# C of the first two pairs by block loads and a VectorE transpose, with other orders around these pairs

## The chip, the cores and the metric

The kernel runs on one core of one Trainium2 chip. The metric is the device time of one execution in microseconds (us). Three runs of the kernel before gave 364.21, 364.57 and 366.34 us; the median is 364.57.

The engines have short names in all tables: PE is TensorE (matrix products), PEld its weight loads, DVE is VectorE, ACT is ScalarE, POOL is GpSimd, and SP is the engine that issues most transfers (DMAs). A name with a q (SPq, DVEq) is the engine's instruction queue.

## The reference

Two stages follow each other. The first is a state-space layer in chunks (4 batches, 8 heads, 768 tokens, head size D = 32, state size N = 16); the second is a two-layer network with a PReLU between its layers.

```python
for c in range(nc):                                  # chunks of 32 tokens
    la = log_a[:, :, sl]; cum = np.cumsum(la, axis=-1)
    L = np.exp(cum[:, :, :, None] - cum[:, :, None, :]) * causal
    M = np.einsum('bhin,bhjn->bhij', Cc, Bc) * L
    y_intra = np.einsum('bhij,bhjd->bhid', M, xc)
    y_inter = np.einsum('bhin,bhnd->bhid', Cc, state) * np.exp(cum)[:, :, :, None]
    y[:, :, sl] = y_intra + y_inter
    Bx = np.einsum('bhjn,bhjd->bhjnd', Bc, xc) * decay_from_j[:, :, :, None, None]
    state = decay_full[:, :, None, None] * state + np.sum(Bx, axis=2)
x = y.transpose(0, 2, 1, 3).reshape(3072, 256)
h = x @ w_in                                         # 256 x 2048
g = np.maximum(h, 0.0) + alpha * np.minimum(h, 0.0)
out = g @ w_out                                      # 2048 x 256
```

The product of C and B of a chunk, before it is multiplied by the decays, is called the gram below. The chunk size of the reference is free: any split of the tokens gives the same result.

## The kernel before

**Tiling.** The 3072 tokens are 24 chunks of 128 tokens, and two neighbouring chunks are a pair (`gp`, 0 to 11). Two pairs, 512 tokens, make a group of the network. Tensor tiles have 128 partitions: B and C with tokens on the partitions (`nat`), or, turned, with head and state index on the partitions (`bc`, whose first half is B and second half is C). `cz` holds C twice, with the odd or the even heads set to zero, so that one matrix product with a 32-row strip gives the gram of two heads. `cd` is C times the decay products `pf`. `dec` holds the decays of a pair, made by scans on VectorE, and is then multiplied by the gram (`times`). `bn` is B times the decays towards the chunk's end; `added` multiplies it with x, and `states` makes the running states from these sums. `mask` sets the parts of a state that belong to other heads to zero. `x_products` and `state_products` give y, and `copy_out` brings it to `xT`, the input of the network.

**The order of work** is written out by hand: every engine runs its instructions in the order in which the program issues them. `first_two` (L818) holds the pairs 0 and 1, in chunks of 64 tokens. It spreads the raw decays to all rows by TensorE (`spread`, into four PSUM banks `sp`), scans them there (`scan`, L867), makes the gram into the other half of the same banks (`gram_of`, L876) and multiplies (`times`, L881). In between it converts the first weight pieces and runs the first parts of the network (`hidden_two`, L1081: two rows of hidden units for 256 tokens; its `rest` is the PReLU, ACT L1099 and DVE L1110). After `first_two` the loop over `f` from 4 to 15 takes the rest of the hidden units of group 0: `hidden(0, f)` (PE L1074, PReLU in ACT L1077 and DVE L1078), the stages of the pairs 2 and 3 (`ssm`), conversions, and `output(f - 4)` (PE L1121). The later groups follow in `quad`.

**Weights** come as 16 pieces of 512 KB, alternating from `w_in` and `w_out`, and each is converted on the way: ACT takes an absolute value (L269), DVE or POOL clamps it (L274), DVE takes the sign (L292), ACT makes a second part (L279, or L282 for `w_out`, which needs `g_mul` and `g_add` from `slope_signs`, L393), DVE combines (L302), and POOL adds (L324). `convert_a`, `sign`, `convert_b` and `convert_next` issue these steps. Six raw buffers exist, and `convert_next` issues the load of a later piece (L253).

**Transfers** are issued by SP in program order, and SP waits where a transfer needs an earlier one. Three results pass through DRAM so that they can be read back to all partitions: `short` (decay products of pair 1; written at L972, read by `load_second`, L227), `z` (decays for the scans of the pairs from 2 on; `rows_out`, L469, read by `load_spread`, L160), and `pf` (decay products from pair 2 on; `rows_products`, L439, read by `load_products`, L167). At pair 2 the state is first multiplied with such a product at L639.

**PSUM** has eight banks: two for tag `hp` (`spare`, `hidden` and the later `quad`), two for `ss`, and four named banks (`bank(0)` to `bank(3)`). `ss_tile` hands out the `ss` buffers and banks in turn by a counter, `early[0]`. Pair 2's gram takes three buffers of `ss_tile` and one of `spare` (`small = 3`).

**Warming.** `keep_warm` issues products without use to keep TensorE busy.

## Time and profile before

The table is of one profiled execution. It took 363.67 us, and its span on the core is 362.0 us.

| stretch, us | PE busy | DVE busy | ACT busy | POOL busy | granted PE clock | DMA share | GB/s |
|---|---|---|---|---|---|---|---|
| 0 to 30.88 | 24.21 | 23.66 | 13.80 | 17.05 | 1.00 | 0.84 | 178 |
| 30.88 to 51.86 | 20.51 | 15.06 | 11.10 | 11.73 | 0.92 | 0.83 | 233 |
| 51.86 to 362.0 | 306.67 | 200.19 | 146.12 | 173.39 | 1.00 | 0.28 | 64 |
| whole | 351.40 | 238.92 | 171.01 | 202.17 | 0.995 | | 84 |

Each row gives the busy time of an engine in a stretch of the span, the share of full speed that TensorE's clock was granted, the mean busy share of the 16 DMA engines, and what they moved. The first stretch ends where `hidden(0, 4)` starts, and the second where `output(4)` starts. A wait is named in the profile by the instruction that waited, an arrow, and the last instruction it seems to have waited for. In the list of an engine's instructions in order of time, the columns are the start, the duration, the engine, the line, the operation, what it writes and reads, and how many are merged into the row.

### The profile page before, as it was taken

To read this page: it belongs to the slowest core of one execution; us is meant where nothing else is said; L and a number is where in the kernel's file an instruction comes from. 1 tells how busy PE (TensorE), PEld (TensorE's weight loads), DVE (VectorE), ACT (ScalarE), POOL (GpSimd) and SP (SyncE) were. 2 spreads that over 40 slices of the span, in tenths; PEclk is the share of its full clock that TensorE was granted. 3 is DMA by queue.
4 is the path that set the end of the run, shared out by engine and by line. 5 is a ranking of instruction groups with operands and counts; after the bars stand their busy time and mean duration, and the time that the engine had idled before them with its cause. 6 is when DMAs were issued, how large, how long until landed. Compare 5 with 4: busy or idle time off the path is not lost.

```text
span 362.0 us, 7766 instructions
## 1 busy us (share of the span) xinstructions
PE 351.4 (97%) x2981; PEld 284.0 (78%) x2981; DVE 238.9 (66%) x489; ACT 171.0 (47%) x386; POOL 202.2 (56%) x224
## 2 busy tenths in 40 slices
PE   7887999999999999999999999999999999999996
PEld 3564656668888888888888888888888888888885
DVE  7976595989846756866656856657856634743363
ACT  3446656544355445535535535535535544453431
POOL 5656457669965947545546545537545546334510
PEclk9998999999999999999999999999999999999999
DMA  6899689704535421510530530530201001001102
GB/s 115 181 188 333 218 179 315 165 2 77 170 66 141 79 53 34 100 45 14 113 82 21 103 84 18 103 86 20 56 2 29 2 2 29 2 0 31 32 0 58
DMA packets 105581, 30.24 MB, mean 84 GB/s; under 512 B 79896, under 2 KB 101448, under 8 KB 105544
## 3 DMA queue, kind: packets, MB, share of 16 engines
q1 hardware_dynamic: 105160, 29.57, 35.6%
q8 instruction: 23, 0.38, 0.4%
q10 hardware_dynamic: 384, 0.18, 0.2%
q14 instruction: 14, 0.11, 0.1%
HBM read 26.32 MB, written 3.42 MB: 82 GB/s over the span
## 4 chain that ended last, share of the span: by engine, by line
PE 86%; DVE 4%; DMA 4%; SPq 2%; POOL 1%; ACT 1%; issue 1%; DVEq 0%; POOLq 0%
PE bank L1195 33%; PE hp L1220 28%; PE bank L1121 6%; PE ss L1220 6%; PE hp L1074 3%; DMA pf<-rpf 2%; PE ss L784 1%; DMA raw<-in_moe_w_in_dram 1%; DVE dec L564 1%; PE ss L728 1%; PE bank L1188 1%; DVE wr L302 1%; PE ss L776 1%; PE ss L802 1%; DMA ap<-pf 1%; POOL w_in L324 1%
## 5 line engine op out<-in xcount | busy, mean ns | idle before, releaser
L1277 POOL TENSOR_TENSOR gt<-gt 128x512 f32<-128x512 f32 x58 | 74.1, 1278 | 21.1 <-DVE gt L1205 16.3
L1195 PE MATMUL bank<-gt,w_out 128*128 128x256 f32 x320 | 83.5, 381 | 0.0
L1195 PEld LDWEIGHTS bank<-gt,w_out 128*128 128x128 f32 x320 | 60.1, 190 | 9.2 <-issue 1.0
L1205 DVE SCALAR_TENSOR_TENSOR gt<-hp,s_mul,gt 128x256 f32<-128x256 f32 x96 | 42.0, 479 | 29.0 <-ACT gt L1203 26.8
L1267 POOL TENSOR_TENSOR gt<-gt 128x512 f32<-128x512 f32 x20 | 25.4, 1269 | 62.6 <-DVE gt L1205 50.2
L1203 ACT ACTIVATE gt<-hp,s_alpha 128x256 f32<-128x256 f32 x96 | 40.3, 471 | 34.6 <-PE hp L1220 31.5
L1195 PE MATMUL bank<-gt,ws 128*128 128x256 f32 x224 | 55.9, 379 | 0.0
L1195 PEld LDWEIGHTS bank<-gt,ws 128*128 128x128 f32 x224 | 42.3, 190 | 5.6
L1220 PE MATMUL hp<-xs,w_in 128*128 128x256 f32 x160 | 41.9, 384 | 0.0
L1220 PE MATMUL hp<-xs,ws 128*128 128x256 f32 x160 | 41.1, 380 | 0.0
L1246 DVE TENSOR_TENSOR hp<-hp,u 128x512 f32<-128x512 f32 x20 | 14.0, 700 | 35.2 <-ACT u L1244 35.2
L1220 PEld LDWEIGHTS hp<-xs,ws 128*128 128x128 f32 x160 | 30.3, 190 | 4.3 <-POOL xs L1162 0.2
L1220 PEld LDWEIGHTS hp<-xs,w_in 128*128 128x128 f32 x160 | 29.7, 190 | 4.5
L1121 PE MATMUL bank<-w_out,gt 128*128 128x256 f32 x128 | 31.1, 385 | 0.4 <-POOL w_out L324 0.4
L1121 PEld LDWEIGHTS bank<-w_out,gt 128*128 128x128 f32 x128 | 23.6, 190 | 7.2 <-issue 3.1
L1074 PE MATMUL hp<-xT,w_in 128*128 128x512 f32 x48 | 24.5, 635 | 2.3 <-DVE gt L1110 2.3
L1220 PE MATMUL ss<-xT,w_in 128*128 128x256 f32 x96 | 24.6, 379 | 0.0
L642 POOL TENSOR_TENSOR sm<-state,bmask 128x256 f32<-128x256 f32 (+1 forms) x10 | 6.2, 621 | 32.1 <-DVE state L639 32.1
L558 DVE TENSOR_TENSOR_SCAN dec<-abc,bank 128x192 f32<-128x192 f32 x48 | 22.7, 523 | 0.0
L1235 ACT COPY m<-hp 128x512 f32<-128x512 f32 x8 | 4.7, 586 | 35.7 <-PE hp L1220 35.7
L1244 ACT COPY u<-hp 128x512 f32<-128x512 f32 x20 | 11.7, 585 | 19.4 <-PE hp L1220 19.4
L1205 DVE SCALAR_TENSOR_TENSOR gt<-c,s_mul,gt 128x256 f32<-128x256 f32 x40 | 20.6, 555 | 0.0
(234 smaller groups left out, 608.0 us busy)
## 6 DMA issues: line engine op xcount, KB each, us to landing
abc<-z SPq DMA_DIRECT2D x24, 192.0 KB
raw<-in_moe_w_in_dram SPq DMA_DIRECT2D x8, 512.0 KB
raw<-in_moe_w_out_dram SPq DMA_DIRECT2D x8, 512.0 KB
abc<-z SPq DMA_DIRECT2D x8, 512.0 KB
out_dram<-o_sb SPq DMA_DIRECT2D x32, 64.0 KB
nat<-in_B_dram SPq DMA_DIRECT2D x26, 64.0 KB
nat<-in_C_dram SPq DMA_DIRECT2D x24, 64.0 KB
xt<-in_x_dram SPq DMA_DIRECT2D x12, 128.0 KB
```

What stands on the lines that cost most here:

```text
L558: nc.vector.tensor_tensor_scan(out=dv[:, o : o + SQ], data0=abc[k][:, s : s + SQ], data1=ident_p[0][:, :SQ], initial=0.0, op0=ALU.mult, op ...
L642: nc.gpsimd.tensor_tensor(out=sm[:, :nk].rearrange("p k (g m) -> p k g m", g=2), in0=new[:, :nk].unsqueeze(2).to_broadcast([P, nk, 2, 2 * D]),
L1074: nc.tensor.matmul(hp, w_in[:, k, f * P : (f + 1) * P], xts[g][:, k], start=(k == 0), stop=(k == KC - 1))
L1121: nc.tensor.matmul(pos[0][t // 2][:, t % 2], gt[:, t * Q : (t + 1) * Q], w_out[:, f], start=(f == 0 and t % 2 == 0), stop=(f == NF - 1), s ...
L1195: nc.tensor.matmul(ms[g][i][:, h], w, blocks[g, z][n][:, p], start=(q == 0 and h == 0), stop=(q == NQ - 1), skip_group_check=True)
L1203: nc.scalar.mul(o[:, p], h[:, p], s_alpha[:, fs[p]])
L1205: nc.vector.scalar_tensor_tensor(out=o[:, p], in0=h[:, p], scalar=s_mul[:, fs[p]], in1=o[:, p], op0=ALU.mult, op1=ALU.max)
L1220: nc.tensor.matmul(to[:, p], w(2 * z + p), b, start=start and p == 0, stop=True, skip_group_check=True)
L1244: nc.scalar.copy(out=u2, in_=A)
L1246: nc.vector.tensor_tensor(out=Y, in0=Y, in1=u2, op=ALU.add)
L1267: nc.gpsimd.tensor_tensor(out=tc_, in0=g22, in1=g12, op=ALU.subtract)
L1277: eng.tensor_tensor(out=o, in0=x0, in1=x1, op=ALU.subtract)
```

## The change

C of the pairs 0 and 1 is no longer loaded with tokens on the partitions in runs of 64 bytes (one token of one head). It is loaded in blocks of 8 tokens of one head, 512 bytes, as the kernel already does for later pairs (`load_blocks`); VectorE then turns 32x32 blocks (`turned_c`), and ScalarE makes `cz` from the turned copy in SBUF (`spread_c`). TensorE still turns B (`turned_b`). `rows_short` is cut in two: the second scan and the write of `short` (`rows_begun`) come after the products of pair 0, with `load_second` and the loads of pair 2 behind them, while the loads of pair 1 go ahead. `gram_of` fills the banks 0 and 1 first. Two clamps and `first_a` of pair 1 go from VectorE to GpSimd, the clamp of weight piece 1 too; the copies of y go from VectorE to ScalarE. `slope_signs` comes earlier. Pair 1's sums, states and gram are issued ahead of `hidden_two(0, 2, 0)` instead of within it. The last `hidden_two` before the loop writes `bank(2)` instead of an `hp` buffer, and the counter of `ss_tile` starts at 17 instead of 16. Two uses of `keep_warm` are shortened or left out.

```diff
--- before.py
+++ after.py
@@ -181,14 +181,25 @@
             load_products(gp, ap)
         if gp == 0:
             load_rows(0, nc.scalar)
-            nc.sync.dma_start(out=al_n, in_=moe_alpha.rearrange("(k p) -> k p", p=P))
         abc = []
         later = []
+        def load_blocks(o, src, e):
+            first = src[b, e : e + 1, c * Q : (c + 2) * Q, :]
+            nc.sync.dma_start(out=o, in_=bass.AP(tensor=first.tensor, offset=first.offset,
+                                                 ap=[[2 * S * N, P // 32], [8 * N, 32], [1, 8 * N]]))
+        for e in range(2 if gp < NB else 0):
+            load_blocks(nat[:, 1, e], C, e)
+        if gp == 0:
+            nc.sync.dma_start(out=al_n, in_=moe_alpha.rearrange("(k p) -> k p", p=P))
         for k in range(2 if gp < HALF else 0):
             ts = slice((c + k) * Q, (c + k + 1) * Q)
-            for i, src in enumerate((B,) if turned else (B, C)):
+            for i, src in enumerate((B,) if turned or gp < NB else (B, C)):
                 nc.sync.dma_start(out=nat[:, i, k].rearrange("p (h n) -> p h n", h=H),
                                   in_=src[b, :, ts, :].rearrange("h p n -> p h n"))
@@ -207,12 +218,8 @@

...
@@ -477,21 +484,24 @@
-    def rows_short(r, rows):
-        clamp(nc.vector, starts_r[:RW, ::HQ], rows[:, ::HQ])
+    def rows_short(r):
         nc.vector.memset(r[:, ::HQ], 0.0)
         pr = lent[3][:RW, 2]
         nc.vector.tensor_tensor_scan(out=pr[:, ::-1], data0=r[:, 1:][:, ::-1],
                                      data1=ends_q[:RW, ::-1], initial=0.0, op0=ALU.mult,
                                      op1=ALU.add)
+        return pr
+    def rows_begun(r):
         rpf = lent[3][:RW, 3]
         nc.vector.tensor_tensor_scan(out=rpf, data0=r[:, :Q], data1=starts_r[:RW], initial=0.0,
                                      op0=ALU.mult, op1=ALU.add)
         scratch["short", 0] = dr.tile([RW, Q], F32, name="short0")
-        held["short"] = rpf
-        return pr
+        nc.sync.dma_start(out=scratch["short", 0], in_=rpf)
     def rows_turn(i, pr):
@@ -831,25 +841,24 @@
-        def turned(nat, tp, by):
-            for i in range(2):
-                for k in range(2):
-                    nc.tensor.transpose(tp[:, (2 * i + k) * P : (2 * i + k + 1) * P],
-                                        nat[:, i, k], ident)
+        def turned_c(nat):
             bc = work.tile([P, 4, Q], F32, name="bc")
+            nc.vector.transpose(
+                bc[:, 2:].rearrange("p k t -> p (k t)").rearrange("p (c b) -> p b c", b=8),
+                nat[:, 1].rearrange("p e (b n) -> p b e n", n=N))
+            return bc
+        def spread_c(bc):
             cz = czp.tile([P, 2, 2, Q], F32, name="cz")
-            flat = bc.rearrange("p i t -> p (i t)")
-            cs = slice(2 * Q, 4 * Q)
-            nc.scalar.copy(out=flat[:, : 2 * Q], in_=tp[:, : 2 * Q])
             for e in range(2):
-                o = cz[:, e].rearrange("p k t -> p (k t)")
-                if e and by is nc.vector:
-                    nc.vector.tensor_scalar(out=o, in0=tp[:, cs], scalar1=par[:, e : e + 1],
-                                            scalar2=None, op0=ALU.mult)
-                else:
-                    nc.scalar.mul(o, tp[:, cs], par[:, e : e + 1])
-            nc.scalar.copy(out=flat[:, cs], in_=tp[:, cs])
-            return bc, cz
+                nc.scalar.mul(cz[:, e].rearrange("p k t -> p (k t)"),
+                              bc[:, 2:].rearrange("p k t -> p (k t)"), par[:, e : e + 1])
+            return cz
+        def turned_b(nat, tp, bc):
+            for k in range(2):
+                nc.tensor.transpose(tp[:, k * P : (k + 1) * P], nat[:, 0, k], ident)
+            nc.scalar.copy(out=bc[:, :2].rearrange("p k t -> p (k t)"), in_=tp[:, : 2 * Q])
@@ -868,14 +877,16 @@
                                          initial=0.0, op0=ALU.mult, op1=ALU.add)
         def gram_of(bc, cz, banks):
-            for k in range(2):
-                for r in range(4):
-                    rs = slice(32 * r, 32 * r + 32)
-                    for j, hs in enumerate(halves):
-                        o = banks[r][hs, (2 + k) * Q : (3 + k) * Q]
-                        nc.tensor.matmul(o.rearrange("p (e t) -> p e t", e=2), bc[rs, k, hs],
-                                         cz[rs, :, k, hs], start=True, stop=True,
-                                         tile_position=(32 * r, HQ * j), skip_group_check=True)
+            for v in range(2):
+                for k in range(2):
+                    for r in (2 * v, 2 * v + 1):
+                        rs = slice(32 * r, 32 * r + 32)
+                        for j, hs in enumerate(halves):
+                            o = banks[r][hs, (2 + k) * Q : (3 + k) * Q]
+                            nc.tensor.matmul(o.rearrange("p (e t) -> p e t", e=2), bc[rs, k, hs],
+                                             cz[rs, :, k, hs], start=True, stop=True,
+                                             tile_position=(32 * r, HQ * j),
+                                             skip_group_check=True)
         def times(i, r, t):
             nc.vector.tensor_tensor(out=dec[i][:, r], in0=t[:, 2 * Q :], in1=dec[i][:, r],
@@ -941,7 +952,7 @@
                 o = xts[0][:, w, 2 * i * Q : 2 * (i + 1) * Q].rearrange(
                     "p (k j t) -> p j k t", k=2, j=2)
                 nc.scalar.copy(out=o[:, 0], in_=y[w][0])
-                nc.vector.tensor_copy(out=o[:, 1], in_=y[w][1])
+                nc.scalar.copy(out=o[:, 1], in_=y[w][1])
@@ -961,89 +972,91 @@
             for c in cs:
                 mask(i, slice(c, c + 1))
         rows = loads["r", 0]
         rq = prep.tile([RW, Q + 1], F32, name="rq")
         clamp(nc.vector, rq[:, :Q], rows)
         z0 = first_a(ap0, nc.vector, lent[1][:, :2])
+        clamp(nc.gpsimd, starts_r[:RW, ::HQ], rows[:, ::HQ])
+        clamp(nc.gpsimd, starts_a[:, ::HQ], ap0[:, ::HQ])
         sp = [bank(r) for r in range(4)]
         spread(z0, sp)
-        prq = rows_short(rq, rows)
-        clamp(nc.vector, starts_a[:, ::HQ], ap0[:, ::HQ])
-        nc.sync.dma_start(out=scratch["short", 0], in_=held.pop("short"))
+        prq = rows_short(rq)
+        bc0 = turned_c(nat0)
         load_pair(1)
-        load_second()
         nat1, _, xt1, pf1 = loads["p", 1]
         for r in range(4):
             scan(0, r, sp[r])
         rows_turn("short", prq)
         tp = spare()
-        bc0, cz0 = turned(nat0, tp, nc.vector)
+        cz0 = spread_c(bc0)
+        turned_b(nat0, tp, bc0)
+        slopes(alpha)
+        bn0 = pair_loads(0)
+        hp = spare()
+        keep_warm(hp, 1)
+        gram_of(bc0, cz0, sp)
+        dps = dps_in([hp, tp])
+        added(dps, bn0, xt0)
+        for r in (0, 1):
+            times(0, r, sp[r])
         nc.vector.tensor_tensor_scan(out=pf0, data0=z0.rearrange("p k t -> p (k t)"),
                                      data1=starts_a, initial=0.0, op0=ALU.mult, op1=ALU.add)
-        bn0 = pair_loads(0)
-        slopes(alpha)
+        z1 = first_a(loads["a", 1], nc.gpsimd, lent[1][:, 2:])
+        cd0 = decayed_c(bc0, pf0)
+        states(0, dps, pf0)
+        one_at_a_time(0, range(3))
+        for r in (2, 3):
+            times(0, r, sp[r])
+        rows_begun(rq)
+        load_second()
         rows_clamp(0)
         rows_out(0)
         load_next(2)
         load_pair(2, False)
         load_next(2)
         load_spread(2, *divmod(4, CPB))
-        cd0 = decayed_c(bc0, pf0)
-        hp = spare()
-        keep_warm(hp, 1, GT)
-        gram_of(bc0, cz0, sp)
-        dps = dps_in([hp, tp])
-        added(dps, bn0, xt0)
-        for r in (0, 1):
-            times(0, r, sp[r])
-        states(0, dps, pf0)
-        one_at_a_time(0, range(3))
-        for r in (2, 3):
-            times(0, r, sp[r])
-        z1 = first_a(loads["a", 1], nc.vector, lent[1][:, 2:])
         convert_a(*pieces[0], by=nc.vector)
         convert_b(*pieces[0])
         y = places([ss(), ss()], [hp, tp])
-        x_products(y, xt0, 0, (0,))
+        x_products(y, xt0, 0)
+        state_products(y, 0, cd0)
         sp = [bank(r) for r in range(4)]
-        keep_warm(sp[0], 1, GT)
-        x_products(y, xt0, 0, (1,))
-        state_products(y, 0, cd0)
         spread(z1, sp)
         keep_warm(sp[3][:, 2 * Q :], 1)
         convert_next()
         xts[0] = xtp.tile([P, KC, GT], F32, name="xT")
         copy_out(0, y)
-        convert_a(*pieces[1], by=nc.vector)
+        prelu_of = {0: hidden_two(0, 0, 0, spare())}
+        convert_a(*pieces[1])
+        bc1 = turned_c(nat1)
+        sign(*pieces[1])
+        scan(1, 0, sp[0])
         convert_b(*pieces[1])
-        prelu_of = {0: hidden_two(0, 0, 0, spare())}
+        for r in range(1, 4):
+            scan(1, r, sp[r])
+        bn1 = pair_loads(1)
+        convert_next(first=False)
+        cz1 = spread_c(bc1)
+        own = [ss(), ss()]
+        turned_b(nat1, own[0], bc1)
+        dps = dps_in(own)
+        added(dps, bn1, xt1)
+        slope_signs()
+        mask(0, slice(3, 4))
+        cd1 = decayed_c(bc1, pf1)
+        states(1, dps, pf1)
+        gram_of(bc1, cz1, sp)
+        one_at_a_time(1, range(3))
         for r in range(4):
-            scan(1, r, sp[r])
-        convert_next(first=False)
-        bn1 = pair_loads(1)
-        mask(0, slice(3, 4))
-        own = [ss(), ss()]
-        bc1, cz1 = turned(nat1, own[0], nc.scalar)
-        dps = [t.rearrange("p (k m) -> p k m", k=2)
-               for t in (own[1][:, 2 * Q : 2 * Q + 4 * D], sp[0][:, : 4 * D])]
-        cd1 = decayed_c(bc1, pf1)
+            times(1, r, sp[r])
+        prelu_of[0]()
+        convert_a(*pieces[2])
+        sign(*pieces[2])
         def among(i, k):
-            if (i, k) == (0, 0):
-                added(dps, bn1, xt1)
-                states(1, dps, pf1)
-            if (i, k) == (0, 1):
-                gram_of(bc1, cz1, sp)
-                one_at_a_time(1, range(3))
-                for r in range(4):
-                    times(1, r, sp[r])
-                prelu_of[0]()
-                convert_a(*pieces[2])
-                sign(*pieces[2])
             if (i, k) == (1, 0):
                 y = places(own, [bank(0), bank(1)])
                 x_products(y, xt1, 1)
@@ -1054,14 +1067,13 @@
         convert_b(*pieces[2])
         convert_next(first=False)
         mask(1, slice(3, 4))
-        slope_signs()
         prelu_of[2]()
         held["pr"] = rows_scan(0)
         rows_products()
         load_products(NB, loads["p", NB][3])
         state[0] = new[1][:, 3]
         masked[0] = sm[1][:, 3]
-        early[0] = 16
+        early[0] = 17
@@ -1418,7 +1430,7 @@
     sign(*pieces[3])
     hidden_two(0, 0, 2 * Q, spare())()
     convert_next(first=False)
-    rest = hidden_two(0, 2, 2 * Q, spare())
+    rest = hidden_two(0, 2, 2 * Q, bank(2))
     rows_turn(0, held["pr"])
     convert_a(*pieces[4])
     rest()
```

More of the change, by code (lines that the diff above doesn't have):

```diff
@@ L211, in load_pair @@
             for e in range(2):
-                first = src[b, e : e + 1, c * Q : (c + 2) * Q, :]
-                nc.sync.dma_start(out=nat[:, 1 + e, i],
-                                  in_=bass.AP(tensor=first.tensor, offset=first.offset,
-                                              ap=[[2 * S * N, P // 32], [8 * N, 32], [1, 8 * N]]))
+                load_blocks(nat[:, 1 + e, i], src, e)
         for k in range(2 if gp >= NB else 0):
```

## The prediction

> **What bounds the kernel now.** I read the waits of TensorE over the whole execution first: they show where the bottleneck engine stands still. The page has it busy for 351.4 of 362.0 us, so only stops can be won. Columns: us in total, times, longest.
>
> ```profile
> PE hp L1074 <- DVE gt L1110: 2.3, 1, 2.3
> PE hp L1089 <- POOL w_in L324: 1.2, 2, 0.9
> PE bank L876 <- DVE gt L904: 0.9, 1, 0.9
> ...
> PE bank L876 <- DVE cz L847: 0.5, 1, 0.5
> PE bank L1121 <- POOL w_out L324: 0.4, 1, 0.4
> ```
>
> All stops lie before 52 us. The last row is the one at 51.4 to 51.86 us, before `output(4)`. From there to the end the groups of TensorE show no other releaser. **So the total is the time at which TensorE gets past 51.86 us, plus 310.1 us that the change doesn't touch.** Second, TensorE in order of time around the largest stop, and the stretches with the granted clock (the number after the busy times, ahead of DMA share and GB/s):
>
> ```profile
> 28.32 0.25 PE L499 MATMUL ss<-ident,pr 96*128 96x96 f32 x1
> 30.88 3.63 PE L1074 MATMUL hp<-xT,w_in 128*128 128x512 f32 x4 [2.32 <-DVE gt L1110]
> ...
> 36.54 1.88 PE L1074 MATMUL hp<-xT,w_in 128*128 128x512 f32 x4
> ```
>
> ```profile
> 32.00:33.00 1.00, 1.00 (x2) 0.42 (x2) 1.00 (x2) 0.09 (x1) 0.92 (x2) 0.50 1.13 339
> 33.00:34.00 1.00, 1.00 (x2) 0.23 (x1) 0.49 (x2) 0.00 (x0) 0.92 (x2) 0.50 1.13 377
> ```
>
> `hidden(0, 4)` waits 2.32 us for its PSUM buffer, then takes 3.63 us instead of 1.88, at half clock: 4.07 us lost in one place. It looks like the prize. Third, the chain of waits from 33 to 52 us says whether it is one:
>
> ```profile
> 33.21 6.02 DMA pf<-rpf
> ...
> 39.24 2.62 DMA ap<-pf
> ...
> 41.96 0.28 DVE state L639
> 42.24 2.33 DVE dec L564 x4
> ...
> 45.69 0.66 DVE gt L1078
> 46.35 2.33 DVE dec L564 x4
> 48.68 0.64 DVE gt L1078
> ...
> 50.53 1.28 POOL w_out L324
> ```
>
> This chain runs beside TensorE. The decay products of pair 2 go out to DRAM, come back to all partitions, and only then can VectorE do pair 2's first state (L639). Behind it, in VectorE's order, stand two sets of scans, two PReLUs (L1078), and the conversion of the weights for `output(4)`, without a gap from 41.96 to 50.46 us. TensorE needs these PReLUs: pair 2's gram for heads 6 and 7 takes the `hp` buffer that the PReLU ending at 46.35 frees (that matmul starts at 46.41), `hidden(0, 8)` the next one. TensorE and this chain arrive within 0.44 us of each other at 51.86. **There are two bounds; shortening only TensorE's side wins 0.44 us at most.**
>
> Fourth, what sets the chain's start. VectorE has `rpf` ready at 27.5 us, but SP issues pf at 33.21. SP in order of time (start, duration):
>
> ```profile
> 9.62 3.48 SPq L192 DMA_DIRECT2D nat<-in_B_dram  x1
> ...
> 17.09 0.43 SPq L253 DMA_DIRECT2D raw<-in_moe_w_in_dram  x1
> ...
> 27.73 3.82 SPq L253 DMA_DIRECT2D raw<-in_moe_w_in_dram  x1
> ```
>
> Other loads of these kinds take 0.4 to 0.6 us, so SP is held inside the issue. The waits name ACT L269 for the 3.82 us, but the raw buffer being reused was last read by ACT at 12.6 us; a full queue fits better. The stretch from 28 to 38 us has a DMA share of 0.98 at 335 GB/s, and from 38 to 40 only 0.04: the queue drains and pf is its last item. So pf lands when the transfers issued since 17.09 us are done; these are seven weight pieces, pair 2's tensors and the spread rows, none of them changed.
>
> **What the Trainium skill says.** "TensorE: Matmul & The Clock Gate", Part 1: the clock halves after an idle window of about 3.4 us and returns after a busy one. The trace agrees on half clock (0.50) for some 3.4 us (0.51 from 31 us, 0.79 in 34 to 35), and shows that a 2.3 us stop was enough. Same page, Architectural detail: VectorE is a strict FIFO; L639 holding up the ready conversions agrees. "DMA: Bandwidth & Descriptors", Specifications: full rate needs 512 bytes per row. Agreed: 95 GB/s at 3 to 6 us (mostly 64-byte rows), 335 GB/s in the stretch above. Same page, Rules for kernel authors: a load of what an earlier DMA wrote waits for its completion; SP waits 5.5 us here for pf before ap.
>
> **The change, part by part.** Times are those of the profiled execution: span 362.0 us, run 363.67, median 364.57 (0.90 above it). I forecast a difference and add it to the median.
>
> *C in blocks.* For pairs 0 and 1, 2 x 2 loads of 64 KB go from 64-byte to 512-byte rows. At the measured rates 128 KB takes 1.35 us at 95 GB/s and 0.39 at 335: about 1 us less DMA per pair. Issues stay six per pair. For pair 0 C is issued first and B about 1 us later, so B's second half lands near 6.8 instead of 6.1 us. The first weight piece is still issued near 6.62 and lands at 11.0 to 11.3 instead of 11.35.
>
> *VectorE's transpose.* Two new ones of 128x256. The nearest row, L571, is 128x512 at 1.11 us; half is 0.55 us each (0.43 to 1.1 as bounds: L1371's 128x256 took 0.43). Removed from VectorE: L847 0.48, two clamps 0.35 + 0.14, pair 1's `first_a` 0.49 (L431, 128x252), piece 1's L274 0.41, four output copies 1.13. Net about 1.9 us less on VectorE. TensorE loses four transposes of C, two warming matmuls of 512 columns (1.03 and 1.13 us). ACT gains four copies of 0.27, loses two of 0.37. POOL gains two small clamps, a 252-wide clamp (0.65 for 127 columns, so 0.7 to 1.3) and piece 1's L274 (0.61); it idles 1.88 and 1.49 us before its L324s there, which covers them.
>
> *Gram 0.* It waited for cz L847 until 8.22. Now: C lands near 4.6, transpose to 5.2, two ACT scalings to 6.5, B's copy to 7.5, gram at 7.6. 0.6 us earlier, hidden behind the first weight piece (usable 14.66, now 14.2 to 14.6).
>
> *Pair 1's loads ahead of `short`; `load_second` after pair 0's times.* `rows_begun` ends near 11 us instead of 4.95. SP then issues `short`, and `load_second` waits for it to land. Queued ahead of `short` are pair 1's B and x, 4096 rows: the same kind of queue that held SP 3.48 us. Before, all of pair 1 was moved by about 17 us; now 1 us less work gives 15.5 to 16. `short` lands 0.4 us later (as ap followed pf's drain), `load_second` takes 0.78, z 0.42 to 1.13: the next weight piece is issued at 16.8 to 18.0 instead of 17.09. Behind it on SP stand all that pf waits for. **Shift of the gate: -0.3 to +0.9 us; I take 0.** The microsecond saved in transfers is spent on an empty queue during the round trip through DRAM. If neither appeared, DMA work alone would allow -1.5.
>
> *Pair 1.* Its ap lands near 18.3 as before, so the states start at 18.6 to 19.3 (18.94). The gram no longer follows them (-0.9 us of TensorE), four products L881 (1.42) and state products follow: xT complete near 23.9 instead of 24.53. -0.6.
>
> *`slope_signs` early, `bank(2)`.* ACT L282 no longer waits 1.90 us for POOL g_add; `hidden(0, 4)` takes a buffer freed one step earlier. The 2.32 us stop and the half clock go. It starts near 27.7, ends at 29.4 at full clock, instead of 34.5: TensorE is about 5 us ahead. Late next: pieces 3 to 5, whose conversions now end at about 29.8, 32.3 and 34.9, when TensorE asks at 29.4, 34.8 and 36.5; 0.4 us of wait. (Piece 3: ACT free of `copy_out` and a PReLU at 24.8, L269 0.6, L282 1.12, a scaling 0.87, then DVE L1110 and L302 to 28.5, POOL L324 1.27; POOL then adds 2.5 us a piece: L274 0.61, L324 1.27, and `bn` of pair 2 once.)
>
> *Where the 5 us go.* TensorE finishes `hidden(0, 7)` near 41, reaches the gram that needs L1078's buffer, and stands until 46.4 + shift: 5 us idle. That is longer than the 2.3 us that halved the clock, so it restarts at half clock. From 46.4 to 51.86 it has 1.0 (gram) + 1.73 (`output(3)`) + 1.96 (`hidden(0, 8)`) of work, with 0.5 us of slack. With 3.4 us at half clock 1.7 us of work are lost, less the slack and the 0.44: **about +0.9 us** (0 if the clock holds, 3.5 if `hidden(0, 8)` is cold too).
>
> Sum: 0 (gate) + 0.9 (cold restart) = +0.9: 364.57 + 0.9 = 365.5.
>
> **Rivals.** A, above: 364.7 to 366.7, chance 0.50. *B, the gate moves a little:* one or two bubbles in the queue vanish (share 0.09 in 25 to 26 us), pf lands up to 1.5 us earlier, the clock mostly holds: 363.0 to 364.7. For it: fewer rows in the queue; against it: `short`'s round trip. 0.25. *C, slower:* `load_second`, at SP's head, waits for `short` behind x of pair 1, the gate moves +1 us or more, and the restart stays cold for over 5 us, through `hidden(0, 8)`: +1 + 3.5 = 369.0, from 366.7 on. It decides from the point where the half clock outlasts the gram and `output(3)`, 5.5 us cold. For it: the stop is twice as long as the one that cost 3.4 us. 0.19, half of it beyond 1%. *D, the chain isn't a bound:* pf is issued as early as ACT or VectorE allow, as the named releaser L269 would mean, and TensorE keeps its 5 us: 359.6. Against it: 0.98 DMA share for ten microseconds. 0.06. *That the gram doesn't get behind the scans* changes nothing: the first weight piece covers it.
>
> **Numbers.** A change within 1% (3.65 us) can't be told from none here. Faster by over 1%: D, 0.06. Slower by over 1%: half of C, 0.10. Within: 0.84. Range 362.9 to 368.0: A, B and the lower part of C.
>
> **What would show it.** Right: `hidden(0, 4)` before 29 us at full clock; ap<-pf landing within 1 us of 41.87; a new wait of TensorE of 4 to 6 us on VectorE's L1078 in the gram L739, followed by clock 0.50. Wrong: pf issued before 31 us, or TensorE passing `output(4)` before 50 us; then DMA was not what held pf.

## The result and the profile after

The changed kernel takes **368.87 us** (median of six runs, 367.42 to 369.94); the kernel before, measured beside it, 364.45 (364.17 to 366.34). The ratio is 1.011, 95% interval 1.007 to 1.014: slower by about 4.4 us, where I had forecast +0.9 and a range that ended at 368.0. All ratios are taken over fast executions alone and lie near the ratio of their means, so for a kernel whose times fall into two groups they differ from the ratio of the medians. The profiled execution after took 369.63 us, 0.76 above its median, the one before 363.67, 0.78 below its own; so the two traces lie 5.9 us apart in span, some 1.5 us more than the medians.

The head of the page after: span, busy times, and the granted clock and DMA share in 40 slices of 9.2 us.

```profile
span 367.9 us, 7755 instructions
PE 355.5 (97%) x2975; PEld 288.2 (78%) x2975; DVE 237.9 (65%) x481; ACT 171.4 (47%) x389; POOL 206.0 (56%) x229
PEclk9799958999999999999999999999999999999999
DMA  5669778920724530430540540540300001001102
```

TensorE has six matmuls fewer in the trace than before and is busy 4.1 us longer. That isn't more work: the clock row shows where its matmuls are stretched, in the second slice (9 to 18 us) and in the sixth and seventh (46 to 64). Next, the largest wait of TensorE after (us in total, times, longest; the second largest is 1.3):

```profile
PE hp L749 <- DVE gt L1090: 3.4, 1, 3.4
```

The 2.3 us stop of `hidden(0, 4)` is gone, and a stop of 3.4 us stands in pair 2's gram, on the PReLU that was L1078 and is L1090 now: the wait that the prediction named as next. TensorE in order of time after shows both ends of it:

```profile
30.32 1.91 PE L1086 MATMUL hp<-xT,w_in 128*128 128x512 f32 x4
...
33.20 1.99 PE L1133 MATMUL bank<-w_out,gt 128*128 128x256 f32 x8 [0.54 <-POOL w_out L331]
...
49.68 0.79 PE L749 MATMUL hp<-cz,bc 32*128 32x256 f32 x1 [3.41 <-DVE gt L1090]
...
51.68 3.78 PE L1133 MATMUL bank<-w_out,gt 128*128 128x256 f32 x8
55.26 2.92 PE L1086 MATMUL hp<-xT,w_in 128*128 128x512 f32 x4
58.01 1.89 PE L1133 MATMUL bank<-w_out,gt 128*128 128x256 f32 x8
```

The end of the same stretch before (gram, `output(3)`, `output(4)`):

```profile
45.68 0.48 PE L739 MATMUL ss<-cz,bc 32*128 32x256 f32 x1
...
46.41 0.48 PE L739 MATMUL hp<-cz,bc 32*128 32x256 f32 x1
...
47.46 1.99 PE L1121 MATMUL bank<-w_out,gt 128*128 128x256 f32 x8
...
51.86 1.99 PE L1121 MATMUL bank<-w_out,gt 128*128 128x256 f32 x8 [0.44 <-POOL w_out L324]
```

`hidden(0, 4)` runs at full clock (1.91 us instead of 3.63), and `output(0)` starts at 33.20, 1.6 us ahead of before. Then all of that is lost and more: `output(4)` starts at 58.01 instead of 51.86. The 6.15 us there are the whole 5.9 us of the span, within 0.3. The chain of waits in the changed kernel says what TensorE stood for:

```profile
36.08 6.28 DMA pf<-rpf
...
42.37 2.77 DMA ap<-pf
...
45.24 0.28 DVE state L649
45.52 2.33 DVE dec L574 x4
...
48.97 0.67 DVE gt L1090
```

It is the chain of before, link by link, from pf to the PReLU. Pair 2's first state starts at 45.24 instead of 41.96, **3.28 us later**. From it to `output(4)` it takes 12.77 us instead of 9.90, **2.87 us more**. So two sums are to be explained. For the second, the granted clock (after the busy time and count of TensorE, ahead of DMA share and GB/s):

```profile
46.00:48.00 2.00, 0.27 (x2) 0.77 0.91 267
48.00:50.00 2.00, 0.32 (x4) 0.50 1.00 314
50.00:52.00 2.00, 2.00 (x11) 0.50 0.54 69
52.00:54.00 2.00, 2.00 (x6) 0.50 0.51 76
54.00:56.00 2.00, 2.00 (x5) 0.50 1.06 127
56.00:58.00 2.00, 2.00 (x4) 0.67 0.39 104
```

Half clock from 47.1 to 57.3 us, through the gram, `output(3)` (3.78 us instead of 1.99) and most of `hidden(0, 8)`. For the first, SP in order of time (start, duration):

```profile
9.02 3.87 SPq L203 DMA_DIRECT2D nat<-in_B_dram  x2
12.94 1.97 SPq L207 DMA_DIRECT2D xt<-in_x_dram  x2
15.03 0.53 SPq L504 DMA_DIRECT2D short<-gt  x1
18.44 0.61 SPq L234 DMA_DIRECT2D ap<-short  x1
19.14 0.41 SPq L476 DMA_DIRECT2D z<-rz  x1
19.60 0.42 SPq L260 DMA_DIRECT2D raw<-in_moe_w_in_dram  x1
```

VectorE has the scan for `short` ready at 12.1 us. SP, held inside the issues of pair 1's B and x, gets to it at 15.03; `ap<-short`, which waits for it to land, goes out at 18.44; the next weight piece, which leads the queue up to pf, at 19.60 instead of 17.09. The waits of SP name this one, and the DMA share shows the queue running empty meanwhile (0.04 from 18 to 20 us):

```profile
SPq L234 <- DMA short<-gt: 2.8, 1, 2.8
```

```profile
16.00:17.00 1.00, 0.65 (x2) 0.50 0.68 127
17.00:18.00 1.00, 1.00 (x3) 0.50 0.09 11
```

The 2.5 us are still there at pf (36.08 instead of 33.21, so 2.9), and another 0.4 is added by the start of the state.

### The profile page after: what moved, and what is told of

The parts are those of the page before. It is cut to its first block, busy times and chain, and to the rows that moved or that the text cites. A ratio compares the mean times of both kernels' runs of the same rounds, so it can differ in the third digit from the quotient of the medians.

```text
span 367.9 us, 7755 instructions
## 1 busy us (share of the span) xinstructions
PE 355.5 (97%) x2975; PEld 288.2 (78%) x2975; DVE 237.9 (65%) x481; ACT 171.4 (47%) x389; POOL 206.0 (56%) x229
## 4 chain that ended last, share of the span: by engine, by line
PE 86%; DMA 6%; SPq 5%; DVE 2%; issue 0%; ACT 0%; POOL 0%; DVEq 0%; POOLq 0%
PE bank L1207 32%; PE hp L1232 28%; PE bank L1133 7%; PE ss L1232 6%; PE hp L1086 4%; SPq L207 2%; DMA pf<-rpf 2%; DMA nat<-in_C_dram 2%; DMA raw<-in_moe_w_in_dram 1%; PE ss L794 1%; PE ss L738 1%; PE bank L1200 1%; PE ss L812 1%; SPq L203 1%; DMA short<-gt 1%; PE ss L786 1%
## 5 line engine op out<-in xcount | busy, mean ns | idle before, releaser
L1232 PEld LDWEIGHTS hp<-xs,ws 128*128 128x128 f32 x160 | 30.3, 190 | 4.3 <-POOL xs L1174 0.2
L1133 PE MATMUL bank<-w_out,gt 128*128 128x256 f32 x128 | 33.0, 402 | 0.5 <-POOL w_out L331 0.5
L1133 PEld LDWEIGHTS bank<-w_out,gt 128*128 128x128 f32 x128 | 24.7, 199 | 8.1 <-issue 3.2
L1086 PE MATMUL hp<-xT,w_in 128*128 128x512 f32 x48 | 23.6, 617 | 0.0
```

What stands on the lines that cost most here:

```text
L1086: nc.tensor.matmul(hp, w_in[:, k, f * P : (f + 1) * P], xts[g][:, k], start=(k == 0), stop=(k == KC - 1))
L1133: nc.tensor.matmul(pos[0][t // 2][:, t % 2], gt[:, t * Q : (t + 1) * Q], w_out[:, f], start=(f == 0 and t % 2 == 0), stop=(f == NF - 1), s ...
L1232: nc.tensor.matmul(to[:, p], w(2 * z + p), b, start=start and p == 0, stop=True, skip_group_check=True)
```

## The experiments

My theory after this reading: (1) `short`'s round trip through DRAM at SP's head moves the gate (the landing of pf, which lets pair 2's state start), (2) the stop that follows costs a long restart at half clock. Rivals: the gate moves for another reason (pieces 1 and 2 now converted elsewhere, or C's loads); the half clock is only seen, not paid for; TensorE's side, stretched at 12.9 to 19.7 us, is the bound.

### Where `short` stands

`e1_short_early` is the kernel after with the old place of `short` alone:

```diff
         prq = rows_short(rq)
+        rows_begun(rq)
         bc0 = turned_c(nat0)
         load_pair(1)
+        load_second()
...
-        rows_begun(rq)
-        load_second()
```

> The changed kernel with the second scan and the write of short back in their old place, ahead of pair 1's loads, and load_second right behind these loads. Theory S (the round trip of short through DRAM, at the head of SP, moves all later loads and with them pf): the third weight piece is issued near 17 us instead of 19.6, ap of pair 2 has landed near 42 instead of 45.2, and the time falls by 2.5 to 4 us to 365 to 366.5. Rival V (the transposes on VectorE, the later halves of B, or the block loads themselves make the start later): no more than 1 us off, 368 to 369.

`e2_before_short_late` is the kernel before with the new place alone (its scan goes from `rows_short` into a `rows_begun` as in the change; the lines from `rows_out` on are moved down, and the cut leaves out where they stood):

```diff
-        nc.sync.dma_start(out=scratch["short", 0], in_=held.pop("short"))
         load_pair(1)
-        load_second()
...
             times(0, r, sp[r])
+        rows_begun(rq)
+        load_second()
+        rows_out(0)
+        load_next(2)
+        load_pair(2, False)
+        load_next(2)
+        load_spread(2, *divmod(4, CPB))
```

> The kernel before, with only the second scan, the write of short, load_second and the SP items behind them moved behind pair 0's products, as the change has them. C is loaded and turned as before. Theory S: the third weight piece is issued 2 to 3 us later than 17.1, the state of pair 2 starts near 44.5 to 45.5 instead of 41.96, TensorE stands about 3 us in pair 2's gram, and the time rises by 3 to 5 us to 367.5 to 369.5. Rival V: within 1 us of the kernel before, 364 to 365.5.

Measured: e1 366.21 us (ratio to before 1.003, 1.000 to 1.006), e2 367.9 (1.012, 1.009 to 1.015). SP in order of time, and VectorE's first state of pair 2, in e1:

```profile
13.60 1.97 SPq L207 DMA_DIRECT2D xt<-in_x_dram  x2
15.66 0.61 SPq L234 DMA_DIRECT2D ap<-short  x1
16.32 0.45 SPq L476 DMA_DIRECT2D z<-rz  x1
16.82 0.96 SPq L260 DMA_DIRECT2D raw<-in_moe_w_in_dram  x1
```

```profile
40.84 0.28 DVE L649 SCALAR_TENSOR_TENSOR state<-gt,ap,ss 128x64 f32<-128x64 f32 x1 [2.62 <-DMA ap<-pf]
```

And the same of e2:

```profile
15.18 0.56 SPq L497 DMA_DIRECT2D short<-gt  x1
19.11 0.60 SPq L227 DMA_DIRECT2D ap<-short  x1
19.81 0.41 SPq L469 DMA_DIRECT2D z<-rz  x1
20.27 0.42 SPq L253 DMA_DIRECT2D raw<-in_moe_w_in_dram  x1
```

```profile
46.10 0.28 DVE L642 SCALAR_TENSOR_TENSOR state<-gt,ap,ss 128x64 f32<-128x64 f32 x1 [3.19 <-DMA ap<-pf]
```

With `short` written early it has landed when SP comes back to it, and the state is at 40.84, 4.4 us earlier than after and 1.1 earlier than before. Put late into the kernel before, it moves the state by 4.1 us (46.10) with nothing else of the change there, and from there to `output(4)` it takes 9.90 us, as before. (1) stands in both directions. In e2 pair 1's states come late too (a 3.6 us wait of TensorE in pair 1's gram), and how much of the 4.1 us comes by that way isn't told apart.

e1 fell into two groups: six of 20 runs at 362.15 to 363.35, fourteen at 365.58 to 367.48, with nothing between. Its profile (362.62) is of the lower one: a stop of 0.7 us in the gram, no half clock behind it, `output(4)` at 50.73. I come back to the upper one.

### What the half clock costs

The first try put useless products into pair 2's gram, ahead of the matmul that stops, to keep TensorE at work:

```diff
                 for r in range(4):
+                    if (gp, k, r) == (NB, 0, 3):
+                        keep_warm(m5_bank[0], 7)
                     rs = slice(32 * r, 32 * r + 32)
```

> The changed kernel with seven products without use (128x256, about 3 us) ahead of the gram product of pair 2 that waits for its buffer. They fill the 3.4 us in which TensorE stands. Theory T (some 2.9 us of the loss are the half clock after this stop): TensorE passes output(4) near 55.2 instead of 58.0, and the time falls by 2 to 3 us to 366 to 367. If the half clock costs nothing because VectorE's chain sets the pace: at most 0.3 us, 368.6. If the products are in the way: 1 us slower.

It failed: 374.36 us (1.029, 1.027 to 1.030). The waits of TensorE in e3 say why:

```profile
PE bank L339 <- DVE dec L574: 5.7, 1, 5.7
```

The bank that I gave them also holds what VectorE's scans read at that time, and the products stood for the scans. `e5_warm_gram` writes the same seven where nobody reads yet:

```diff
+                        keep_warm(gram[0][:, 1].rearrange("p h t -> p (h t)"), 7)
```

> The changed kernel with seven products without use (128x256) ahead of the gram product of pair 2 that waits for its buffer; they write to the part of the gram's own first bank that is overwritten next, which VectorE isn't reading (in e3_warm they wrote to the bank of the identity and waited for VectorE's scans). Theory T (the half clock after the stop costs about 2.9 us): the clock stays at full speed or drops for one window at most, TensorE passes output(4) near 55 instead of 58, 365.5 to 367. If the half clock is no part of the loss: 368 to 369.

Measured 367.35 us (1.009, 1.006 to 1.012). TensorE in order of time:

```profile
50.30 0.48 PE L751 MATMUL hp<-cz,bc 32*128 32x256 f32 x1 [0.17 <-DVE gt L1092]
51.36 1.99 PE L1135 MATMUL bank<-w_out,gt 128*128 128x256 f32 x8
53.36 1.96 PE L1088 MATMUL hp<-xT,w_in 128*128 128x512 f32 x4
55.75 1.99 PE L1135 MATMUL bank<-w_out,gt 128*128 128x256 f32 x8 [0.43 <-POOL w_out L331]
```

Full clock from 22 us on, and `output(4)` 2.26 us earlier (55.75), although the state is 0.6 us later (45.86) than after. From state to `output(4)` it is 9.89 us, and before it was 9.90. So in the trace the restart costs 2.87 us, all of the second sum. In the medians it is only 1.0 (set against each kernel's own runs of before) to 1.5; gate and clock differ from run to run. The 3.4 us that e5 keeps over before go with the gate, which is as late in it as after.

### Is the chain of pf the bound, and was it before?

In `e4_pf_early` pair 2's decay products are scanned and written behind z, where their data is ready, and read back before the spread rows; the conversion of the first weight piece is issued ahead of them, and nothing else of the kernel after is changed. `e6` does the same to the kernel before. `e7` gives the kernel before only what frees TensorE's prefix (its work up to `hidden(0, 4)`). `e8` does both.

```diff
+        convert_a(*pieces[0], by=nc.vector)
+        convert_b(*pieces[0])
         load_second()
         rows_out(0)
+        rows_products()
         load_next(2)
         load_pair(2, False)
         load_next(2)
+        load_products(NB, loads["p", NB][3])
         load_spread(2, *divmod(4, CPB))
...
-        rows_products()
-        load_products(NB, loads["p", NB][3])
```

```diff
         convert_next()
+        slope_signs()
         xts[0] = xtp.tile([P, KC, GT], F32, name="xT")
...
         mask(1, slice(3, 4))
-        slope_signs()
...
-        early[0] = 16
+        early[0] = 17
...
-    rest = hidden_two(0, 2, 2 * Q, spare())
+    rest = hidden_two(0, 2, 2 * Q, bank(2))
```

The first is of e4 (in e6 and e8 the same block in the other order of lines), the second of e7 and e8.

> The changed kernel with the decay products for pair 2 scanned behind the first weight piece and written to DRAM right behind z, and read back behind the fifth and sixth weight piece. If the landing of these products is the gate: the state of pair 2 starts before 40 us, TensorE has no stop over 1 us in pair 2's gram, passes output(4) near 50, and the time falls to 361.5 to 363.5, below the kernel before. If something else holds TensorE there (the PReLUs, the weight pieces): 366 to 369.

> The kernel before with pf written right behind z and read back behind the fifth and sixth weight piece; nothing else is moved. If there are two bounds within 0.44 us of each other, as the prediction said: TensorE's side (the 2.3 us stop and the half clock from 31 us) is now the only one, and the gain is 0.4 to 1 us, 363.2 to 364. If the wait for pf were the whole loss: 361 to 362.

> The kernel before with bank(2) for the last hidden_two, the counter at 17, and slope_signs behind the first weight piece. TensorE loses its 2.3 us stop and runs hidden(0, 4) at full clock. With pf as second bound: hidden(0, 4) starts near 28.5, TensorE then stands 3 to 5 us in pair 2's gram; the time is between 0.4 us faster and 3 us slower than the kernel before, 363.8 to 367. If TensorE's side alone were the bound: 4 us faster, 360.

> Both together: the kernel before with bank(2), slope_signs early, and pf early. Both bounds are gone, so the gains don't add but multiply in sight: hidden(0, 4) near 28.5, no stop in the gram over 1 us, output(4) near 48.5 instead of 51.86, 360.5 to 362. If a third bound (weight pieces, conversions) follows at once: 363 to 364.

| kernel | median us | ratio to before (95%) | state of pair 2 | stop in its gram | `output(4)` |
|---|---|---|---|---|---|
| after | 368.87 | 1.011 (1.007 to 1.014) | 45.24 | 3.4 | 58.01 |
| e4 | 361.56 | 0.994 (0.992 to 0.996) | 38.92 | none | 49.16 |
| e6 | 361.45 | 0.993 (0.990 to 0.995) | 38.09 | none | 48.55 |
| e7 | 365.22 | 1.003 (1.001 to 1.005) | 42.81 | 2.9 | 52.70 |
| e8 | 359.49 | 0.988 (0.984 to 0.992) | 37.87 | none | 48.24 |

The last three columns are from the traces, in us. With pf out of the queue (e4) the state waits for nothing, and the changed kernel gets 7.0 us faster (each set against its own runs of before), though `short` still stands late: the chain of pf is the bound after. e7 frees TensorE's prefix as the change does (`hidden(0, 4)` at 29.75, full clock) and wins nothing. Its largest wait of TensorE, and the clock there (after busy time and count):

```profile
PE hp L739 <- DVE gt L1078: 2.9, 1, 2.9
```

```profile
46.00:48.00 2.00, 0.75 (x9) 1.00 1.15 284
```

The stop has only moved, and in this trace no half clock follows it: from state to `output(4)` it takes 9.89 us. So the chain was a bound before, too. e6 gains 2.5 us without touching TensorE's side, more than I thought possible. Its trace has the prefix stop of before, nearly to the tenth, and no half clock behind it:

```profile
30.82 1.96 PE L1074 MATMUL hp<-xT,w_in 128*128 128x512 f32 x4 [2.22 <-DVE gt L1110]
```

In the kernel before the half clock comes and goes, too. Of its 103 executions beside the experiments (a far outlier of 370.05 us left out), the 22 with a mean clock of 0.998 or more took 363.7 us in the median, the 50 at 0.994 to 0.995 (as the trace of before, with its one window at half clock) 363.8, and the 31 with a lower clock 365.1. So one window cost little or nothing there, since pf was late anyway; more of it goes with 1.3 us.

### C's part alone

`e11_c_alone` is the kernel before with C of both pairs in blocks, VectorE's transpose, and `cz` from it, and no other order changed (`load_blocks`, `turned_c`, `spread_c` and `turned_b` are those of the change):

```diff
+        bc0 = turned_c(nat0)
...
-        bc0, cz0 = turned(nat0, tp, nc.vector)
+        cz0 = spread_c(bc0)
+        turned_b(nat0, tp, bc0)
...
+        bc1 = turned_c(nat1)
...
-        bc1, cz1 = turned(nat1, own[0], nc.scalar)
+        cz1 = spread_c(bc1)
+        turned_b(nat1, own[0], bc1)
```

> The kernel before with only C's loads in blocks, VectorE's transposes and the scalings from SBUF; all orders, short and the warming products as before. The prediction's reading: about 1 us less transfer time per pair moves the landing of pf forward by 0.3 to 1.2 us and TensorE's side stays, so 363.3 to 364.5 (before 364). Rival V (transposes and late B cost more than they bring): 365 to 367.

364.52 us (1.001, 0.998 to 1.004): no difference that can be told, though a loss of 1.4 us or a gain of 0.7 would not show. Its trace has `hidden(0, 4)` with the old 2.33 us stop and half clock, and the state at 41.32. The part that the change is named for does nothing that these runs can measure.

### The two groups of e1

> e1 with the two warming products of 512 columns put back in the first 12 us. If the half clock from 10 to 20 us is what makes the upper group: one group, near 362.5. If the upper group comes from the stop in the gram or from pf: two groups remain, as TensorE only gets there earlier and stands longer.

`e15` is e1 with the two 512-column products that kept TensorE warm in the kernel before:

```diff
-        keep_warm(hp, 1)
+        keep_warm(hp, 1, GT)
...
-        x_products(y, xt0, 0)
-        state_products(y, 0, cd0)
+        x_products(y, xt0, 0, (0,))
         sp = [bank(r) for r in range(4)]
+        keep_warm(sp[0], 1, GT)
+        x_products(y, xt0, 0, (1,))
+        state_products(y, 0, cd0)
```

It shortens the half clock of the prefix to one window (16 to 19 us) and took 366.66 us (1.002, 0.999 to 1.005), the groups blurred but both there (361.65 to 367.94), and its profile (366.13) is of the upper end:

```profile
PE hp L749 <- DVE gt L1092: 3.3, 1, 3.3
```

```profile
48.66 3.78 PE L1135 MATMUL bank<-w_out,gt 128*128 128x256 f32 x8
52.23 2.42 PE L1088 MATMUL hp<-xT,w_in 128*128 128x512 f32 x4
54.49 1.89 PE L1135 MATMUL bank<-w_out,gt 128*128 128x256 f32 x8
```

Its state is at 42.22, 1.4 us later than e1's; the stop is 3.3 us, and half clock follows for 6.8. Two further single executions of e1's kernel (`e13`, `e14`) fill in between:

> e1 again, for a trace of the upper group. If the upper group is the half clock behind the stop in pair 2's gram: a span near 364.5, a wait of TensorE over 1.5 us there, and clock 0.50 for 3.4 us or more from 45 us on. If it is a later landing of pf: state of pair 2 near 44 us instead of 40.84, with full clock.

| execution | us | state | stop | half clock behind it | `output(4)` |
|---|---|---|---|---|---|
| e1 | 362.62 | 40.84 | 0.7 | none | 50.73 |
| e14 | 363.03 | 41.29 | 1.0 | none | 51.19 |
| e13 | 364.17 | 41.88 | 1.8 | 3.4 us | 52.56 |
| e15 | 366.13 | 42.22 | 3.3 | 6.8 us | 54.49 |
| after | 369.63 | 45.24 | 3.4 | 10.2 us | 58.01 |

A later gate makes a longer stop (e15's is longer still since its TensorE arrives earlier), and in these executions from 1.8 us on half clock comes on top: 1.4 us of gate become 3.8 at `output(4)`. From state to `output(4)` it takes 9.9 us in e1 and e14, 10.68 in e13 with one window of 3.4 us at half clock, 12.27 in e15 with two and 12.77 after with three. Nothing of this is a cost of its own beside the two sums above. It can split one kernel into two groups, but no trace of e1's own upper group was taken, and the mean clocks of its executions fit only in part. Eleven of the fourteen upper ones are at 0.975 to 0.981, below all but one of the lower (five at 0.986, one at 0.980). The other three, at 367.29 to 367.48 us, are at 0.990: less half clock in all than in any of the lower group. So the cause of the two groups isn't shown.

> As e13, a second try for the upper group, with the same two readings.

> e1 (short early), whose times fall into two groups, 362.2 to 363.4 and 365.6 to 367.5, with two products without use (128x256, 0.9 us) in the stop ahead of pair 2's gram. If the upper group are executions in which this stop halves the clock: one group only, 362 to 363.5. If the groups come from elsewhere: both remain.

Two useless products in e1's gram (`e12_short_early_warm`) did not remove the upper one: 366.08 us (1.003, 0.999 to 1.006), three of 12 runs low. By what I had expected of it, that speaks for another cause. But seven of the nine upper runs have mean clocks of 0.975 to 0.980, as in e1, so two products may just have been too few to keep the clock up. What moves the landing of pf by 1.4 us from one execution to the next stays open. So do the single worths of the change's other orders (the gram by banks, the clamps on GpSimd, the copies on ScalarE): they were not tried one by one. e1, which keeps all of them, has pair 2's state earlier than before.

### The version that beats both

> The changed kernel with short early (as e1), pf early (as e4) and the two warming products of 512 columns that the change left out. If the chain through DRAM and the half clock were all that was wrong with the change: the rest of it is worth something, TensorE runs at full clock from 7 us on, and the time is below the best so far, 357.5 to 359.5. If the rest brings nothing over two small edits of the kernel before (e8): 359.5 to 361.

> e4 (pf early) with the two warming products put back, and short left late. If the half clock in the first 20 us, which appears with the shorter warming, delays pair 1's products: hidden(0, 4) starts 1 us earlier than in e4's 30.09, and the time falls by 0.5 to 1.5 us to 360 to 361. If it is hidden behind the waits for short and the weight pieces: within 0.4 us of e4's 361.56.

`e9` is the kernel after with `short` early, pf early and the two warming products back: 359.6 us (0.987, 0.981 to 0.992; 357.97 to 362.04). TensorE in its trace:

```profile
27.83 1.91 PE L1088 MATMUL hp<-xT,w_in 128*128 128x512 f32 x4
...
46.23 1.90 PE L1135 MATMUL bank<-w_out,gt 128*128 128x256 f32 x8
```

`output(4)` comes 5.6 us ahead of before. e8, two small edits of the kernel before, has the same median within its spread (359.49); the two can't be told apart. `e10`, e4 with the warming alone, took 361.55 (0.992, 0.989 to 0.995), as e4, with `hidden(0, 4)` at 30.19 instead of 30.09: behind the late `short` the half clock of the first 20 us is hidden (one window of it remains in e10's trace, three in e4's).

## Why the prediction was wrong, point by point

**Right: the structure.** Two bounds; the prefix stop and its half clock vanish and the time doesn't fall with them; the next stop is in pair 2's gram on this PReLU, half clock behind it. That "shortening only TensorE's side wins 0.44 us at most" held in e7, which won nothing. What happened is rival C (369.0), to which I gave 0.19; its mechanism and its two terms are those measured. That its 369.0 is so near the 368.87 is luck in part: its +1 for the gate was too small (3.4 in the medians, 3.28 in the traces), and its 3.5 for the clock too large (1.0 to 1.5, and 2.87).

**The step that failed** is "`short` lands 0.4 us later (as ap followed pf's drain), `load_second` takes 0.78, z 0.42 to 1.13: the next weight piece is issued at 16.8 to 18.0 instead of 17.09", and with it "Shift of the gate: -0.3 to +0.9 us; I take 0". The queue drained near 16.8 us (share 0.68 in 16 to 17, 0.09 in 17 to 18), a microsecond after my 15.5 to 16. Then `load_second` went out only at 18.44, some 1.6 us after the drain, not 0.4. The trace of before could have told: by the lines I used, the queue was empty from 38 us and ap followed at 39.24, which is 1.2. `load_second` and z took no longer than I said (0.61 and 0.41), and the piece went out at 19.60. The gate moved by +3.28, 2.5 of it at this piece; e1 and e2, which move only `short` and what stands behind it, shift it by 4.4 and 4.1.

**Mis-sized: the cold restart.** I took one window of 3.4 us at half clock, less the slack: +0.9. (I wrote the slack as 0.5 and 0.44; from the same figures it is 51.86 less 46.4 less 4.69 of work, 0.77, with the 0.44 in it, and only that gives 0.9.) One window does cost about this: 0.78 in e13. In the trace after it was three, 10.2 us, and +2.87 (e5 removed it), where my 3.5 for "`hidden(0, 8)` is cold too" was the nearer end. By the medians of after and e5 it is 1.0 to 1.5, so what this term costs in a usual execution stays open between the two. The stop itself was 3.4 us, not 5: TensorE came to the gram less far ahead.

**Wrong, at no cost: TensorE's lead.** I had `hidden(0, 4)` at 27.7; it started at 30.32. Two things held it back, and undoing one gave at most 1.1 us. With the two warming products back but `short` late (e10) it starts at 30.19; with `short` early but no such products at 29.2 to 30.3 (e1, e12 to e14); with both at 28.86 (e15) and, with pf early as well, at 27.83 (e9). I had counted the two products as time saved and put the clock that they hold up at nothing, without a reason. As the chain of pf set the end, e10 shows no price for it.

**Too small: the other bound's worth.** From arrivals 0.44 us apart I read, for e6 as well, that either side alone could win about that much. e6 won 2.5 by the chain alone. The two arrivals were not independent: in the trace of before TensorE itself waits for the chain in the gram (46.41, on the PReLU that ends at 46.35), and from the gram's start to `output(3)` it takes 1.78 us instead of 1.08 in e6. Of the 3.31 us by which e6's trace has `output(4)` earlier, 1.70 lie between `hidden(0, 4)` and `output(0)`, where this execution lacks the half clock; the other 1.6 lie behind, mostly in and after the gram. The half clock is there in some executions only, and the trace I read had it. That "a 2.3 us stop was enough" is true of that trace; in e6 2.22 us was not, and in e7 2.9.

**Right: C's part.** I gave the blocks and transposes no net effect on the end; e11 measured 1.001. VectorE's transposes took 0.64 and 0.65 us, against 0.55 taken and 1.1 as the upper bound.

## What to carry to other kernels

Before shortening an engine's path, follow the chain that arrives at the same time on the other side; here the change removed a visible 4 us from the side that didn't decide. A write that is read back through DRAM should be issued as soon as its data exists and stand well ahead of its reader in the queue: one such pair at the head of SP held up everything behind it for 3.4 us, and moving the next one forward was worth 2.5 us in the kernel before and 7.0 in the changed one. Price a stop of TensorE with the restart that may follow it, here from none to three windows and from 0 to 2.9 us.

## What the runs showed that I had not expected

A longer stop doesn't always cost the clock, and a shorter one can. After 2.3 us it halved in the trace of before and after 2.22 us it didn't in e6; after 1.8 us it halved in e13, and after 2.9 us it didn't in e7, whose mean clock is 1.000 over the whole span. The Trainium skill, "TensorE: Matmul & The Clock Gate", Part 1, calls the window free-running and the cold stretch variable from run to run. The traces agree: read in slices of 1 us (a slice with a mean clock of c spends 2(1 - c) us at half clock), the clock switches at 13.0, 19.8, 47.1 and 57.3 us after, at 9.7, 20.0, 47.3 and 50.7 in e13, and at 15.8, 19.2, 46.5 and 53.3 in e15. Within each execution these times lie whole multiples of 3.41 us apart, within 0.05, and the series starts elsewhere in each. So it is likely to matter how a stop falls on these windows. The stops of before (28.6 to 30.9) and of e13 (44.5 to 46.3) lie wholly inside one, at whose end the clock fell. In e6 and e7 the clock doesn't switch anywhere near, so whether their stops were split between two isn't visible.

The same page also says that full clock returns after at least one busy window of about 3.4 us. In e13 one was enough. In the trace after TensorE is busy without a gap from 50 us, through the whole window from 50.5 to 53.9, and half clock lasts until 57.3, so there one wasn't. That window begins in the gram, with matmuls of 32 rows; whether that is why was not tested.

In e3 the useless products waited 5.7 us for VectorE's reads from the same PSUM bank. That this was the bank and not the elements was not tested.
